# Three fp32 warm-up products in place of nine bfloat16 ones, and state buffers handed out by turn of use

## The chip, the cores and the metric

The kernel runs on one core of a Trainium2 chip. The metric is the device time of one launch in microseconds, the median of several runs. A core has a matrix engine (TensorE, PE in the profile, with PEld for its weight loads), a vector engine (VectorE, DVE), a scalar engine (ScalarE, ACT), GpSimd (POOL) and SyncE (SP), which here issues nearly all loads. They run side by side and wait for each other by semaphores; each works through its own queue in order.

## The reference, cut to what matters

Two layers: a linear attention with a decaying state, and a gated feed-forward block. B, H, S, D are 4, 8, 768, 48; the block has 3072 tokens of 384 values and 1536 hidden units.

```python
for t in range(S):
    kt, vt, rt, wt = (k[:, :, t], v[:, :, t], r[:, :, t], w[:, :, t])
    cur = np.einsum('bhd,bhe->bhde', u[None] * kt, vt)
    y[:, :, t] = np.einsum('bhd,bhde->bhe', rt, state + cur)
    state = wt[:, :, :, None] * state + np.einsum('bhd,bhe->bhde', kt, vt)
...
gate = 1.0 / (1.0 + np.exp(-(x @ w_gate)))
val = x @ w_val
return (gate * val @ w_out).astype(np.float32)
```

Here x is the attention's output with the heads of a token side by side.

## The kernel before, in words

**Attention.** The sequence is cut into six chunks of 128 steps, and a chunk of one batch entry is a group q; there are 24 groups, and group q works on batch entry q % 4 and chunk q // 4. For a group, SyncE loads a decay tile (`load_pin`, with w, k and r in lanes) and a token tile (`load_tok`, with r, v and k in rows). VectorE scans the decays and scales k and r (`prep_k`, L396 to L402; `prep_r`, L413 and L418). TensorE turns the scaled k (`turn_k`, L428), ScalarE copies it (`take_k`, L432), and ScalarE also squares the scans to watch their bounds (`guard`, L423). The scans lie in the tile `eg`, of which there is one, so the scan of the next group waits for `guard` of this one. `scores_sums` makes the scores (L447) and the sums of k and v over half chunks (L550); `mask` puts the scores into the tile `att` (L538); `state_mix` multiplies r with the states (L461) and the scores with v (L574). The bonus with u is made by GpSimd: `bonus1` (L366) and `bonus2` (L369) multiply, VectorE reduces (`bonus3`, L373), GpSimd multiplies again (`bonus4`, L386 and L387), and for the first four groups TensorE adds it to the result (`add_bonus`, L582).

**The state in two steps.** `fade` (L408) writes the state, faded to the start of a chunk, into `ready[q]`. `middle` writes the state at mid-chunk into `mid[q]` (ScalarE at L559 for the first four groups, VectorE at L561 for the others), and `keep` (L565) writes the state at the end of the chunk. `ready` and `mid` have two buffers each, made once, and a group's buffer is picked when its step is written. Readers of both are the products of `state_mix` (L461) and, for groups 12 and on, of `turned` (L484).

**Feed-forward.** The weights stay in SBUF after being taken apart into a high and a low part (`fetch`, `w_top` L286, `w_body` L297, `w_join` L301, `w_hi` L324, `w_lo` L327). `gate` and `value` (L632 and L635) make the hidden units, `sigmoid`, `hidden`, `hidden_hi` and `hidden_lo` (L646, L653, L660, L664) prepare them, and `down` or `down_turned` (L675, L679, L700) makes the output.

**Order.** The first half is written out by hand in the string ORDER: a list of steps, each of which goes to the queues of its engines in that order. Its first line is

```python
first pin0 pk0 pin1 pr0 tk0 st512 tok0 kT0 ub guard0 pk1 tok1 ss0 st256 words4 pr1 tk1 st512 m00 b1_1 m10 kT1 words0 b1_0 mid0
```

`pin0`, `tok0` and `words4` are loads; `pk0`, `pr0`, `tk0`, `kT0`, `ss0`, `b1_0` are the steps above for group 0. `first` and the steps `st512` and `st256` issue products that nobody reads (`stir`, L741), into the bank "pu". Those of `st512` and `st256` read `ends`, a tile of ones and zeros on 112 partitions; those of `first` read `blank`, a zeroed tile in the place of the tag "junk" (L267 and L268). The groups are not visited in the order of their numbers: 0 to 7, then 11, 8, 9, 10, then 12 and on, both for `fade` and for `middle`. The second half is the loop at L786, in which each of 48 steps does a block of hidden units for 512 tokens, with the next groups' work laid between.

Of the kernel before, what the change touches and what calls it, by code (L numbers as in the profile page):

```python
# [8 lines left out]
F32 = mybir.dt.float32  # L9
F32R = mybir.dt.float32r  # L10
BF16 = mybir.dt.bfloat16
# [10 lines left out]
P = 128  # L22
# [189 lines left out]
def tile_kernel(ctx: ExitStack, tc: tile.TileContext, dec: bass.AP, tok: bass.AP, wts: bass.AP, u: bass.AP, out: bass.AP):  # L212
    nc = tc.nc
# [3 lines left out]
    p1 = own.enter_context(tc.tile_pool(name="p1", bufs=1))  # L217
# [38 lines left out]
    ub = const.tile([P, DM], F32, name="ub")  # L256
# [7 lines left out]
    tiny = const.tile([1, 24], F32, name="tiny")  # L264
    nc.vector.memset(tiny, 0.0)
    nc.scalar.activation(tiny, tiny, AF.Sigmoid)
    blank = p1.tile([P, 2, 516], BF16, tag="junk", name="blank")[:, 0]  # L267
    nc.vector.memset(blank, 0.0)  # L268
    state = [const.tile([L, NP, D], F32, name=f"state{b}") for b in range(B)]

# [1 line left out]
    mids, readies = ([const.tile([L, NP * D + REST], F32, name=f"{n}{i}") for i in range(2)] for n in ("mid", "ready"))  # L272
# [57 lines left out]
    pin, tk, eg, bon, kT, att, ready, mid, bank, x, xf, gap = {}, {}, {}, {}, {}, {}, {}, {}, {}, {}, {}, {}  # L330
# [27 lines left out]
    def by_pair(t):  # L358
        return t[:, :NP * D].rearrange("a (p d) -> a p d", d=D)
# [43 lines left out]

    def fade(q):

        ready[q] = readies[q % 2]
        end = eg[q][:, 1:389:W1].unsqueeze(2).broadcast_to([L, NP, D])
        nc.vector.tensor_tensor(out=by_pair(ready[q]), in0=state[q % B], in1=end, op=ALU.mult)  # L408

# [144 lines left out]

    def middle(q):

        mid[q] = mids[q % 2]
        if q < B:
            nc.scalar.copy(by_pair(mid[q]), bank["v", q, 0])  # L559
        else:  # L560
            nc.vector.tensor_tensor(out=by_pair(mid[q]), in0=bank["v", q, 0], in1=by_pair(ready[q]), op=ALU.add)  # L561
# [65 lines left out]
    def up(s, side, n, f, i0, i1):  # L627
        t = ps1.tile([P, 512], F32, tag=side, name=f"{side}{n}_{i0}_{f}")[:, :(i1 - i0) * C]
        for k in range(NKT):
            cols = slice(s * DM + k * P, s * DM + (k + 1) * P)  # L630
            if n == 0 and (i0, f) in WHOLE:
                nc.tensor.matmul(t, lhsT=fulls[f].bitcast(F32)[:, cols], rhs=xf[n, i0][:, k], start=k == 0, stop=k == NKT - 1)  # L632
                continue
            for j, (w, a) in enumerate(((wlo, 0), (whi, 1), (whi, 0))):
                nc.tensor.matmul(  # L635
                    t, lhsT=w[f][:, cols], rhs=x[n][:, a, k, i0 * C:i1 * C], start=k == 0 and j == 0, stop=k == NKT - 1 and j == 2)
        return t
# [3 lines left out]
    def gate(n, f, i0, i1):  # L641
        hid["g", n, f, i0] = up(0, "pg", n, f, i0, i1)
# [95 lines left out]
    def stir(lhs, rhs):  # L738

        t = ps1.tile([P, 512], F32, tag="pu", name="stir")[:, :rhs.shape[1]]  # L740
        nc.tensor.matmul(t, lhsT=lhs, rhs=rhs, start=True, stop=True)  # L741

    ahead = (2, 0, 0, B)
    todo = {"ub": lambda: nc.sync.dma_start(ub, u.partition_broadcast(P)), "ahead": lambda: gate(*ahead), "first": lambda: [stir(blank[:, :P], blank[:, :512]) for _ in range(9)]}
    for cols in (256, 512,):
        todo[f"st{cols}"] = lambda cols=cols: stir(ends[:, :P], ends[:, :cols])

# [3 lines left out]
    for q in range(3 * B + 2):  # L751
        for kind, f in (
            ("pin", load_pin), ("tok", load_tok), ("b1_", bonus1), ("b2_", bonus2), ("b3_", bonus3), ("b4_", bonus4),
            ("pk", prep_k), ("fade", fade), ("pr", prep_r), ("guard", guard), ("tk", turn_k), ("kT", take_k), ("ss", scores_sums),
            ("mid", middle), ("keep", keep), ("sx", state_mix), ("yb", add_bonus), ("tx", turn_x), ("xf", plain_x), ("xh", take_x), ("xl", rest_x),
        ):
            name(f"{kind}{q}", f, q)
        for o in range(2):
            name(f"m{o}{q}", mask, q, o)
            name(f"y{o}{q}", take_y, q, o)  # L760
# [25 lines left out]
    for n in range(2, NC_):  # L786
        for f in range(NFF):
            a = (n, f, 0, B)
# [15 lines left out]
            if nxt == 3 * B + 1:  # L804
                prepare((bonus1, bonus2, prep_k, fade), nxt)
            elif nxt is not None and lag == 1:
                prepare((bonus1, bonus2), nxt)
# [12 lines left out]
            if cur is not None:  # L820
                scores_sums(cur)
                middle(cur)
                mask(cur, 0)
                mask(cur, 1)
                if cur < NG - B:
                    keep(cur)
# [13 lines left out]
            if nxt == 3 * B + 1:  # L840
                prepare((bonus3, bonus4, prep_r, guard), nxt)
            elif nxt is not None and lag == 1:
                prepare((prep_k, fade), nxt)
# [49 lines left out]
```

## Time and profile before

| what | us |
|---|---|
| median of three runs | 559.24 (558.42 to 560.91) |
| profiled execution, all of it | 559.54 |
| its span, from the first to the last instruction | 557.8 |
| TensorE busy | 543.8 |
| VectorE busy | 333.6 |
| ScalarE busy | 254.2 |
| GpSimd busy | 108.8 |

The busy time is a sum over the span; engines overlap. The page also cuts the span into 40 slices and gives the busy tenths of each engine in each. In the timeline a row gives the start in us, the duration, the engine, the line, the operation, what it writes and reads, how many are merged into it, and in brackets the idle time of the engine just before, with what ended it. A row with several products gives the time from the start of the first to the end of the last. An fp32 product of `stir` shows as two instructions.

### The profile page before, as it was taken

To read this page: it belongs to the slowest core of one execution; us is meant where nothing else is said; L and a number is where in the kernel's file an instruction comes from. 1 tells how busy PE (TensorE), PEld (TensorE's weight loads), DVE (VectorE), ACT (ScalarE), POOL (GpSimd) and SP (SyncE) were. 2 spreads that over 40 slices of the span, in tenths; PEclk is the share of its full clock that TensorE was granted. 3 is DMA by queue.
4 is the path that set the end of the run, shared out by engine and by line. 5 is a ranking of instruction groups with operands and counts; after the bars stand their busy time and mean duration, and the time that the engine had idled before them with its cause. 6 is when DMAs were issued, how large, how long until landed. Compare 5 with 4: busy or idle time off the path is not lost.

```text
span 557.8 us, 13756 instructions
## 1 busy us (share of the span) xinstructions
PE 543.8 (97%) x5875; PEld 455.5 (82%) x5875; DVE 333.6 (60%) x550; ACT 254.2 (46%) x598; POOL 108.8 (20%) x104
## 2 busy tenths in 40 slices
PE   8799999999999999999999999999999999999996
PEld 3578889999888888888888788888788888888884
DVE  6899999886634444865765665765656633321122
ACT  2556635433221323646646645645656555411221
POOL 2561520321003102331231211321311300000000
PEclk9999999999999999999999999999999999999999
DMA  8994382221310231334244344155343322100001
GB/s 292 417 386 198 144 311 87 101 101 43 115 58 1 102 139 62 116 133 141 89 147 147 113 163 162 61 164 161 116 165 120 102 65 60 63 0 2 0 1 59
DMA packets 20658, 68.46 MB, mean 123 GB/s; under 512 B 3057, under 2 KB 6769, under 8 KB 19057
## 3 DMA queue, kind: packets, MB, share of 16 engines
q1 hardware_dynamic: 17856, 63.22, 32.3%
q10 hardware_dynamic: 2736, 4.33, 2.1%
q8 instruction: 47, 0.77, 0.6%
q14 instruction: 19, 0.15, 0.1%
HBM read 61.63 MB, written 4.72 MB: 119 GB/s over the span
## 4 chain that ended last, share of the span: by engine, by line
PE 87%; DVE 5%; ACT 3%; DMA 2%; issue 1%; POOL 1%; SPq 1%; ACTq 0%; DVEq 0%; POOLq 0%
PE pg L635 24%; PE pu L635 24%; PE po L700 17%; PE po L679 7%; PE pt L484 2%; PE pa L447 2%; DMA tok<-tok 2%; PE pa L550 2%; PE po L675 1%; PE pk L428 1%; PE pa L574 1%; PE pu L632 1%; PE pa L461 1%; PE pg L632 1%; PE px L596 1%
## 5 line engine op out<-in xcount | busy, mean ns | idle before, releaser
L635 PE MATMUL pg<-x,w 128*128 128x512 f32 (+1 forms) x702 | 156.3, 367 | 0.9 <-ACT sq L317 0.7
L635 PE MATMUL pu<-x,w 128*128 128x512 f32 (+1 forms) x702 | 155.6, 366 | 0.0
L635 PEld LDWEIGHTS pg<-x,w 128*128 128x128 f32 x702 | 121.6, 188 | 23.1 <-ACT sq L317 1.1
L635 PEld LDWEIGHTS pu<-x,w 128*128 128x128 f32 x702 | 122.1, 188 | 21.7
L653 DVE TENSOR_TENSOR sg<-pu,sg 128x512 f32<-128x512 f32 (+1 forms) x84 | 51.5, 613 | 139.0 <-PE pu L635 133.4
L646 ACT ACTIVATE sg<-pg 128x512 f32<-128x512 f32 (+1 forms) x84 | 45.2, 538 | 129.5 <-PE pg L635 120.8
L660 ACT CAST hh<-sg 128x512 fp32r<-128x512 f32 (+1 forms) x75 | 42.6, 570 | 106.1 <-DVE sg L653 106.1
L700 PE MATMUL po<-hh,w 128*128 128x512 f32 x288 | 88.7, 390 | 0.0
L366 POOL TENSOR_TENSOR bon<-tok,ub 128x384 f32<-128x384 f32 x24 | 33.2, 1386 | 242.1 <-DMA tok<-tok 168.1
L664 DVE TENSOR_TENSOR hl<-sg,hh 128x512 fp32r<-128x512 f32 (+1 forms) x78 | 51.9, 671 | 41.1 <-ACT hh L660 38.7
L700 PEld LDWEIGHTS po<-hh,w 128*128 128x128 f32 x288 | 54.1, 188 | 11.0
L700 PE MATMUL po<-hl,w 128*128 128x512 f32 x144 | 57.4, 399 | 0.0
L679 PE MATMUL po<-w,hh 128*128 128x384 f32 x168 | 42.9, 336 | 0.0
L396 DVE TENSOR_TENSOR_SCAN eg<-pin,ends 112x516 f32<-112x516 f32 x24 | 33.7, 1405 | 6.2 <-DMA pin<-dec 4.3
L369 POOL TENSOR_TENSOR bon<-bon,tok 128x384 f32<-128x384 f32 x24 | 32.0, 1337 | 1.6
L700 PEld LDWEIGHTS po<-hl,w 128*128 128x128 f32 x144 | 27.0, 188 | 6.1 <-DVE hl L664 0.2
L381 POOL TENSOR_TENSOR at<-same,a 128x512 f32<-128x512 bf16 x12 | 22.2, 1851 | 44.4 <-DVE a L373 44.4
L679 PEld LDWEIGHTS po<-w,hh 128*128 128x128 f32 x168 | 30.5, 188 | 0.3
L413 DVE TENSOR_TENSOR_SCAN eg<-pin,heads 112x516 f32<-112x516 f32 x24 | 30.3, 1263 | 0.0
L423 ACT ACTIVATE junk<-eg 112x1032 bf16<-112x1032 f32 x24 | 25.5, 1061 | 8.5 <-DVE eg L413 8.5
L679 PE MATMUL po<-w,hl 128*128 128x384 f32 x84 | 29.3, 349 | 0.0
L418 DVE TENSOR_TENSOR pin<-pin,eg 112x512 f32<-112x512 f32 x24 | 25.5, 1062 | 0.8
(111 smaller groups left out, 621.2 us busy)
## 6 DMA issues: line engine op xcount, KB each, us to landing
pin<-dec SPq DMA_DIRECT2D x23, 772.0 KB, 6.1
tok<-tok SPq DMA_DIRECT2D x24, 576.0 KB, 7.3
seen<-wts SPq DMA_DIRECT2D x36, 384.0 KB, 3.1
wraw<-wts SPq DMA_DIRECT2D x12, 1151.6 KB, 10.5
y<-o ACTq DMA_DIRECT2D x10, 256.0 KB, 2.0
y<-o ACTq DMA_DIRECT2D x8, 192.0 KB, 2.0
x<-gap SPq DMA_DIRECT2D x72, 16.0 KB, 4.0
pin<-dec SPq DMA_DIRECT2D x1, 512.0 KB, 3.6
```

The source lines that it names most:

```text
L366: nc.gpsimd.tensor_tensor(out=bon[q][:, :DM], in0=tk[q][:, 0:DM], in1=ub, op=ALU.mult)
L369: nc.gpsimd.tensor_tensor(out=bon[q][:, :DM], in0=bon[q][:, :DM], in1=tk[q][:, 2 * DM:], op=ALU.mult)
L396: nc.vector.tensor_tensor_scan(out=e[:, 516:0:-1], data0=t[:, 516:0:-1], data1=ends[:, 516:0:-1], initial=0.0, op0=ALU.mult, op1=ALU.add,)
L413: nc.vector.tensor_tensor_scan(out=e[:, WW:WW + 516], data0=t[:, 0:516], data1=heads[:, 0:516], initial=0.0, op0=ALU.mult, op1=ALU.add,)
L418: nc.vector.tensor_tensor(out=rr(q), in0=rr(q), in1=er, op=ALU.mult)
L635: nc.tensor.matmul(t, lhsT=w[f][:, cols], rhs=x[n][:, a, k, i0 * C:i1 * C], start=k == 0 and j == 0, stop=k == NKT - 1 and j == 2)
L646: nc.scalar.activation(sg, hid["g", n, f, i0], AF.Sigmoid)
L653: nc.vector.tensor_tensor(out=sg, in0=hid["u", n, f, i0], in1=sg, op=ALU.mult)
L660: nc.scalar.copy(hh, hid["s", n, f, i0])
L664: nc.vector.tensor_tensor(out=hl, in0=hid["s", n, f, i0], in1=hid["hi", n, f, i0].bitcast(F32), op=ALU.subtract)
L679: nc.tensor.matmul(po[n, i][:, :DM], lhsT=h[:, c], rhs=w[f][:, 2 * DM:], start=f == 0 and j == 0, stop=f == NFF - 1 and j == 2,)
L700: nc.tensor.matmul(po[n, k], lhsT=w[f][:, cols], rhs=h, start=f == 0 and j == 0, stop=f == NFF - 1 and j == 2)
```

## The change

The tile `blank` is read as fp32: 516 words of 4 bytes on each partition, all of them cleared. `first` issues three products of 128 by 512 fp32 in place of nine of the same shape in bfloat16. `ready` and `mid` take their two buffers in turn of use, by how many groups have had one, in place of the parity of the group's number. Since group 11 is visited between 7 and 8, this changes the buffer of groups 8 to 11 alone: 11 and 9 now have buffer 0, 8 and 10 buffer 1; before it was the other way round.

```diff
-    blank = p1.tile([P, 2, 516], BF16, tag="junk", name="blank")[:, 0]
+    blank = p1.tile([P, 2, 516], BF16, tag="junk", name="blank").rearrange("a i c -> a (i c)").bitcast(F32)
     nc.vector.memset(blank, 0.0)
...
     def fade(q):
 
-        ready[q] = readies[q % 2]
+        ready[q] = readies[len(ready) % 2]
...
     def middle(q):
 
-        mid[q] = mids[q % 2]
+        mid[q] = mids[len(mid) % 2]
...
-    todo = {..., "first": lambda: [stir(blank[:, :P], blank[:, :512]) for _ in range(9)]}
+    todo = {..., "first": lambda: [stir(blank[:, :P], blank[:, :512]) for _ in range(3)]}
```

More of the change, by code (lines that the diff above doesn't have):

```diff
@@ L743, in tile_kernel @@
     ahead = (2, 0, 0, B)
-    todo = {"ub": lambda: nc.sync.dma_start(ub, u.partition_broadcast(P)), "ahead": lambda: gate(*ahead), "first": lambda: [stir(blank[:, :P], blank[:, :512]) for _ in range(9)]}
+    todo = {"ub": lambda: nc.sync.dma_start(ub, u.partition_broadcast(P)), "ahead": lambda: gate(*ahead), "first": lambda: [stir(blank[:, :P], blank[:, :512]) for _ in range(3)]}
     for cols in (256, 512,):
```

## The prediction

> **What bounds the kernel now.** I read the page first: where each engine is idle, slice by slice (a slice is 557.8/40 = 13.9 us).
>
> ```profile
> span 557.8 us, 13756 instructions
> PE 543.8 (97%) x5875; PEld 455.5 (82%) x5875; DVE 333.6 (60%) x550; ACT 254.2 (46%) x598; POOL 108.8 (20%) x104
> ...
> PE   8799999999999999999999999999999999999996
> ...
> DMA  8994382221310231334244344155343322100001
> ```
>
> TensorE is busy nearly everywhere; its 14 us of idle time lie mostly in the first two slices and the last one. The change's products run in the first slice, so what matters is which resource sets the first 30 us. The busy time by stretch (PE, PEld, DVE, ACT, POOL, granted clock, DMA share, GB/s) and then the chain of waits answer it.
>
> ```profile
> 8.00:10.00 2.00, 2.00 (x18) 0.50 (x21) 0.48 (x1) 1.48 (x3) 0.00 (x0) 1.00 0.89 168
> ...
> 16.00:18.00 2.00, 0.15 (x10) 0.15 (x10) 1.66 (x3) 1.07 (x2) 2.00 (x3) 1.00 1.00 415
> ```
>
> VectorE alone, from its start at 16.34 to TensorE's at 32.53 (busy time, granted clock, DMA share, GB/s):
>
> ```profile
> 16.34:32.53 16.19, 15.97 (x21) 1.00 1.01 420
> ```
>
> The chain of waits:
>
> ```profile
> 3.24 9.55 DMA tok<-tok
> ...
> 12.94 2.30 POOL bon L366 x2
> ...
> 15.30 1.01 POOL bon L369
> ...
> 16.34 0.55 DVE a L373
> ...
> 32.57 1.56 PE pu L632 x6
> ```
>
> The chain begins with the second token load, issued at 3.24 and landed at 12.79 because the DMA engines are full. It frees GpSimd's two bonus multiplies at 12.94, then its third at 15.30, and at 16.34 VectorE's reduction of them. From there VectorE is busy 15.97 of 16.19 us, and only then does TensorE take over. No first product stands in this chain. It stands beside it, in the timeline:
>
> ```profile
> 1.05 0.27 DVE L268 MEMSET blank<- 128x258 uint32 x1
> 1.38 5.73 PE L741 MATMUL stir<-blank 128*128 128x512 bf16 x9 [1.38 <-DVE blank L268]
> ...
> 5.09 0.66 DVE L402 TENSOR_TENSOR pin<-pin,eg 112x512 f32<-112x512 f32 x1
> 6.91 0.95 PE L428 MATMUL pk<-ident,pin 112*128 112x112 f32 x4
> 6.93 0.69 DVE L418 TENSOR_TENSOR pin<-pin,eg 112x512 f32<-112x512 f32 x1
> 7.66 1.94 PE L741 MATMUL stir<-ends 112*128 112x512 f32 x2
> 7.90 0.53 ACT L432 COPY kT<-pk 128x448 f32<-128x448 f32 x1 [5.49 <-PE pk L428]
> 8.33 1.07 ACT L423 ACTIVATE junk<-eg 112x1032 bf16<-112x1032 f32 x1
> ...
> 9.52 1.23 DVE L396 TENSOR_TENSOR_SCAN eg<-pin,ends 112x516 f32<-112x516 f32 x1 [1.89 <-ACT junk L423]
> 11.60 0.60 PE L428 MATMUL pk<-ident,pin 112*128 112x112 f32 x4
> 12.04 1.04 PE L741 MATMUL stir<-ends 112*128 112x512 f32 x2
> 12.72 0.69 DVE L418 TENSOR_TENSOR pin<-pin,eg 112x512 f32<-112x512 f32 x1
> 14.13 0.36 DVE L565 TENSOR_TENSOR state<-pa,mid 112x192 f32<-112x192 f32 x1
> 16.34 0.55 DVE L373 TENSOR_REDUCE a<-bon 128x8 f32<-128x384 f32 x1 [1.85 <-POOL bon L369]
> 17.85 0.36 PE L574 MATMUL pa<-tok,at 64*32 64x48 f32 x11 [1.93 <-issue]
> ```
>
> Here is a second path: the ninth product ends at 7.11, the transposes of group 0 (pk) could have begun at 5.75 when L402 ended but begin at 6.91, ScalarE copies them (kT), runs the bounds square of L423 behind that, and VectorE waits 1.89 us for it, since there is one eg buffer. So the first products do hold VectorE's group 1. But that path ends at 14.49 with the state update of L565, and VectorE then sits idle for 1.85 us until GpSimd's multiply. Those 1.85 us are the cover of the whole edit.
>
> **The change, part by part.**
>
> The blank memset. Before, it clears 258 words a partition in 0.27 us; now it clears 516, twice as many, so 0.27 x 516/258 = 0.55. The first product starts about 0.27 later, at 1.65. VectorE's first operation that the first products could hold up, L402, comes at 5.09, so only TensorE feels it.
>
> The first products. Nine bfloat16 ones go: 5.73 us. Three fp32 ones of 512 columns come; the nearest rows are the existing stirs on ends, of the same type and length, each of which shows as two instructions. One takes 1.94 us at 7.66 and 1.04 us at 12.04. The same instruction at two speeds means that the array is still slow at 7.66, though the granted clock reads 1.00 in the 8 to 10 row. Ends: if the three run at the slow rate, 3 x 1.94 = 5.82, ending at 7.47, 0.36 later than 7.11. If they all ran fast, 3 x 1.04 = 3.12, ending at 4.77; then pk starts at 5.75, when its data is there, takes 0.60 in place of 0.95, kT runs 6.4 to 6.9, the square cannot start before the scan that it reads is done, just ahead of L418 at 6.93, and VectorE's second scan follows the square's start by 9.52 - 8.33 = 1.19 as now, so at 8.12 in place of 9.52: 1.40 earlier. I take the slow end, since the slow row is the nearest in time (7.66, against 12.04), and treat the path as 0.36 later.
> [...]
>
> What lies behind it. The late end moves VectorE's L565 end from 14.49 to 14.85, 1.49 us before the multiply that it waits for next; the early end moves it to 13.09 and the idle time grows to 3.2. Both cost or bring 0. If that cover were gone, the price would be the shift itself: +0.36 or -1.40. TensorE's six fewer instructions of loads and products (18 become 12) move the place where it starves at 16 to 18 us (the 1.93 us before the last 11 products of L574, attributed to issue), by six instructions. That place is under VectorE's gapless work too. SP's queue: the change issues no DMA; SP's third decay load waits for TensorE's L461 and moves with it, as the next rows show, and the weight loads queue behind it.
>
> ```profile
> 15.23 0.33 SPq L341 DMA_DIRECT2D pin<-dec  x1
> ...
> 24.55 1.23 DVE L396 TENSOR_TENSOR_SCAN eg<-pin,ends 112x516 f32<-112x516 f32 x1
> ```
>
> Its reader starts at 24.55 without a wait, 9.3 us after the issue, and the DMA share at 16 to 18 is 1.00, so an issue 0.4 later or 1.4 earlier keeps its place in a full line: 0. GpSimd's queue gets nothing new.
>
> GpSimd beside VectorE. The only way in which the shift touches the chain is through the two multiplies of 12.94 to 15.24, which overlap L418 and VectorE's next operations. Their durations (least, median, most, in ns):
>
> ```profile
> L366 POOL TENSOR_TENSOR bon<-tok,ub x24: 995/1278/1992, 12.9 to 436.1; 128x384 f32<-128x384 f32 x24
> ```
> ```profile
> L369 POOL TENSOR_TENSOR bon<-bon,tok x24: 998/1339/2607, 15.3 to 437.8; 128x384 f32<-128x384 f32 x24
> ```
>
> The pair takes 2.30. At the minimum it would be 1.99 (-0.31), at the maximum 3.98 (+1.68). A VectorE path 0.36 later overlaps about as much as before, so I take 0 and keep both for the range.
>
> The state buffers. mid and ready now take turns in the order in which groups are visited (0 to 7, then 11, 8, 9, 10, 12 on), so group 11 no longer takes the buffer of group 7, nor 12 that of 10. What that could remove is a wait of fade (L408) or middle (L561) for products of the group before:
>
> ```profile
> L408 DVE TENSOR_TENSOR ready<-state,eg x20: 344/352/1169, 50.0 to 438.1; 112x192 f32<-112x192 f32 x20
> its engine sat idle before it (us, times) until:
> who waited for it (us, times):
> ```
> ```profile
> 204.47 0.35 DVE L408 TENSOR_TENSOR ready<-state,eg 112x192 f32<-112x192 f32 x1
> ```
> ```profile
> 202.43 0.22 PE L461 MATMUL pa<-mid,pin 48*64 48x48 f32 x2
> ```
> ```profile
> DVE mid L561 <- PE pa L550: 6.8, 11, 2.5
> ```
>
> The list of what L408 waited for is empty. Group 11's, at 204.47, comes 1.8 us after the last reader of the old buffer (202.65). The waits of L561 are for L550, the products that it takes in, and none is for L461, the readers of a buffer. So nothing is removed, and behind group 12 both rules give the same parity: 0. What is late next is what was late before.
>
> **Sum.** 0 (memset and products under 1.85 us of cover) + 0 (GpSimd pair) + 0 (buffers) = 0 against the profiled execution, 557.8 of span and 559.54 in all, which lies 0.30 above the median of 559.24. I predict the median, 559.2.
>
> **The rivals.** The faster one: the early end is real and the chain is wrong about what holds VectorE at 16.34, so that the 1.40 us carry through, with 0.31 of GpSimd's pair: 559.2 - 1.7 = 557.5. For it speaks the 1.89 us wait of VectorE for ScalarE, which the first products cause; against it, that the wait is followed by the 1.85 us one for GpSimd, whose own wait is for a load in a full DMA. It is 0.3%, still under what would count as faster; for that 2.8 us would have to go, and TensorE's path holds no more than 1.40.
>
> The slower one: VectorE's displaced two-input operations collide with GpSimd's multiplies on the chain. It decides from the first overlap, as the pair is on the chain without slack. At their maxima the pair costs 1.68 more and the third multiply 2.61 - 1.01 = 1.60 more: 559.2 + 3.3 = 562.5, 0.6% slower. For it speak the spread of those rows; against it, that VectorE is idle during the third multiply now and would still be, and that a shift of 0.36 keeps the pair's overlap.
> [...]
>
> A third: TensorE starves longer at 16 to 18 us because its instructions end elsewhere. The products that follow (L582) go to ScalarE, whose copy of them stands ahead of its cast of a weight (L324), and that cast feeds VectorE's L327:
>
> ```profile
> 20.28 0.81 PE L582 MATMUL pa<-bon,ident 128*128 128x192 f32 x4
> ...
> 21.03 1.16 ACT L324 CAST w<-full 128x1152 fp32r<-128x1152 f32 x1
> ...
> 22.61 1.35 DVE L327 TENSOR_TENSOR w<-full,w 128x1152 fp32r<-128x1152 f32 x1
> ```
>
> ScalarE's cast ends at 22.19 and VectorE needs it at 22.61, so it decides from 0.42 us on; a starving time twice as long gives 1.93 - 0.42 = +1.5, 560.7. Nothing makes six instructions cost that much, so it is unlikely.
>
> **How the numbers follow.** About 0.5% of 559.2, 2.8 us, is what a measurement of this kernel can tell from no change; its three runs alone lie between 558.42 and 560.91. No change: 0.80, 558.2 to 560.2. Faster rival: 0.10, at 557.5. Third: 0.05, at 560.7. Collision: 0.05, at 562.5. The range 557.4 to 560.8 takes in all but the last and some spread of the runs. Over 0.5% faster (under 556.4): 0.05, from a faster rival with a fast set of runs; over 0.5% slower (above 562.0): 0.05, the collision; within: 0.90.
>
> **What the profile would show.** Right: three pairs of fp32 products from 1.65 to about 7.4 (or earlier, if they run fast), pk and the square moved by the same, VectorE's idle time before 16.34 changed by the opposite amount, the second token load landing near 12.8, and TensorE's first long stretch beginning near 32.5. L408 and L561 lie as before. Wrong: if GpSimd's pair starts at 12.9 but VectorE's reduction does not start near 16.3, or if the second token load lands at another time than 12.8, or if TensorE's slow rate outlives 10 us and VectorE's group 1 comes more than 1.85 us late.

## The result and the profile after

The changed kernel takes 563.03 us (median of seven runs, 561.57 to 563.96) against 559.24 (seven runs, 558.42 to 562.21). The ratio is 1.0056, 95% interval 1.0032 to 1.0079: slower by about 3 us (3.8 by the two medians), and outside the predicted range. Its profiled execution took 562.21 with a span of 560.4, against 559.54 and 557.8, so the two traces hold about 2.6 us of the loss. Single runs spread: of 75 runs of the kernel before that were timed beside the experiments, the 8 with a mean granted clock under 0.9935 have a median of 562.1 us and the 49 at 0.9965 or more one of 559.0, and all seven of the changed kernel lie between 0.991 and 0.996.

The page of the changed kernel:

```profile
span 560.4 us, 13750 instructions
...
PE   7789999999999999999999999999999999999996
...
PEclk9899999999999999999999999999999999999999
```

TensorE lost a tenth in the first slice and in the third and, new, the granted clock dips in the second (14.0 to 28.0 us). Behind that TensorE's digits are as before. The chain of waits of the changed kernel shows what stands there now (start, duration, what):

```profile
14.45 0.61 PE pa L461 x15
15.05 0.73 PE pa L574 x56
15.78 3.66 issue
19.44 0.29 PE pa L574 x7
19.73 1.55 PE stir L741 x2
21.28 0.04 issue
21.33 2.07 PE stir L741 x2
23.40 0.49 PE pa L582 x2
...
23.92 0.32 ACT bon L587
24.24 1.06 ACT w L324
...
32.42 1.96 DVE eg L396
...
36.10 1.56 PE pu L632 x6
```

Before, the chain went through the token load, GpSimd and VectorE here. Now it goes through TensorE: a hole of 3.66 us, then warm-up products that nobody reads, then the bonus products, ScalarE's cast, VectorE. The timeline of the changed kernel, to be read against the rows shown before:

```profile
1.10 0.49 DVE L268 MEMSET blank<- 128x516 f32 x1
1.65 5.67 PE L741 MATMUL stir<-blank 128*128 128x512 f32 x6 [1.65 <-DVE blank L268]
7.16 0.55 PE L428 MATMUL pk<-ident,pin 112*128 112x112 f32 x4
7.54 1.04 PE L741 MATMUL stir<-ends 112*128 112x512 f32 x2
9.36 1.23 DVE L396 TENSOR_TENSOR_SCAN eg<-pin,ends 112x516 f32<-112x516 f32 x1 [1.61 <-ACT junk L423]
12.56 0.69 DVE L418 TENSOR_TENSOR pin<-pin,eg 112x512 f32<-112x512 f32 x1
12.71 2.35 POOL L366 TENSOR_TENSOR bon<-tok,ub 128x384 f32<-128x384 f32 x2 [8.53 <-DMA tok<-tok]
13.31 0.70 PE L447 MATMUL pa<-pin 48*64 48x64 f32 x32 [0.39 <-DVE pin L418]
16.18 0.55 DVE L373 TENSOR_REDUCE a<-bon 128x8 f32<-128x384 f32 x1 [1.85 <-POOL bon L369]
19.44 0.29 PE L574 MATMUL pa<-tok,at 64*32 64x48 f32 x8 [3.66 <-issue]
19.66 3.74 PE L741 MATMUL stir<-ends 112*128 112x512 f32 x4
23.20 1.01 PE L582 MATMUL pa<-bon,ident 128*128 128x192 f32 x4
24.13 1.16 ACT L324 CAST w<-full 128x1152 fp32r<-128x1152 f32 x1
25.32 1.36 DVE L327 TENSOR_TENSOR w<-full,w 128x1152 fp32r<-128x1152 f32 x1 [2.79 <-ACT w L324]
```

Up to 16.2 us VectorE's and GpSimd's rows agree with those of before within 0.25 us. Then TensorE is without instructions for 3.66 us in place of 1.93. The warm-up products behind the hole stood like this before, in the timeline and in the stretches (PE, PEld, DVE, ACT, POOL, granted clock, DMA share, GB/s):

```profile
18.14 2.31 PE L741 MATMUL stir<-ends 112*128 112x512 f32 x4
```
```profile
18.00:20.00 2.00, 1.94 (x15) 0.78 (x8) 2.00 (x4) 1.25 (x1) 2.00 (x3) 1.00 1.00 423
20.00:22.00 2.00, 2.00 (x56) 1.51 (x58) 1.90 (x4) 1.23 (x3) 1.43 (x2) 1.00 1.04 431
```

They now hold up the bonus products by 23.20 - 19.66 = 3.54 in place of 20.28 - 18.14 = 2.14, because the clock has dropped; the stretches of the changed kernel show it:

```profile
18.00:20.00 2.00, 0.56 (x9) 0.45 (x9) 2.00 (x4) 0.56 (x1) 2.00 (x3) 1.00 1.01 420
20.00:22.00 2.00, 1.94 (x3) 0.50 (x2) 1.90 (x4) 0.71 (x1) 1.27 (x2) 0.54 1.02 429
22.00:24.00 2.00, 2.00 (x6) 1.05 (x4) 0.53 (x1) 0.08 (x1) 0.00 (x0) 0.60 0.98 408
```

The sum: the hole ends 1.52 later at the first warm-up product (19.66 against 18.14), the products there cost 1.40 more, so the bonus products start 2.92 later. ScalarE's cast starts 3.10 later (24.13 against 21.03); VectorE had 0.42 to spare for it, which leaves 2.68, and VectorE is seen to wait 2.79. The span grew by 2.6. That the 2.68 comes near this is in part luck. A later scan of `eg` by VectorE takes 0.81 longer, 1.96 in the chain above (at 32.42) against this row in the chain of before:

```profile
29.70 1.15 DVE eg L396
```

So TensorE's long stretch begins 36.10 - 32.57 = 3.53 later. About 1 us of that is won back between 100 and 400 us, in part because waits of TensorE that the kernel before has there (0.7 and twice 0.2) are gone and only one of 0.3 is new. Why the scan was slower is not shown; GpSimd's multiply beside it took 2.19 in place of 1.90.

Why is the hole longer? The records of the DMA queue that carries instructions hold 47 packets of 16 KB beside 11,837 TensorE records in the kernel before, one for every 252; below, a block is what one such packet brings. Around the hole there is one such packet, the first of that queue. The row of that queue (packets, MB, share of the 16 engines) in the kernel before, in the stretch 15 to 16 us:

```profile
q8 instruction: 1, 0.02, 6.2%
```

and of the changed kernel in the stretch 17 to 18 us:

```profile
q8 instruction: 1, 0.02, 6.4%
```

By the trace's times the packet starts at 15.40 before and at 17.11 after, 1.71 later. Counted in order of time from 0, TensorE's instruction behind the hole is number 449 in both, and it starts 2.45 and 2.33 us after the packet does. In the kernels below this distance is 2.29 to 2.45, and 2.93 in e11. From this near-constant distance I take the starving to be a wait for a block of code, and the block comes later after the change.

### The profile page after: what moved, and what is told of

Its sections match the earlier page's. It is cut to its first block, busy times and chain, and to the rows that moved or that the text cites. A ratio compares the mean times of both kernels' runs of the same rounds, so it can differ in the third digit from the quotient of the medians.

```text
span 560.4 us, 13750 instructions
## 1 busy us (share of the span) xinstructions
PE 544.1 (97%) x5872; PEld 456.0 (81%) x5872; DVE 333.2 (59%) x550; ACT 253.6 (45%) x598; POOL 109.2 (19%) x104
## 4 chain that ended last, share of the span: by engine, by line
PE 89%; ACT 4%; DVE 3%; issue 2%; DMA 2%; ACTq 0%; SPq 0%; DVEq 0%
PE pg L635 25%; PE pu L635 24%; PE po L700 16%; PE po L679 8%; PE pa L447 2%; PE pt L484 2%; PE pa L550 2%; PE pa L574 2%; PE po L675 1%; PE pk L428 1%; PE pa L461 1%; PE pu L632 1%; PE pg L632 1%; PE stir L741 1%; DMA x<-gap 1%
## 5 line engine op out<-in xcount | busy, mean ns | idle before, releaser
L366 POOL TENSOR_TENSOR bon<-tok,ub 128x384 f32<-128x384 f32 x24 | 31.7, 1322 | 239.1 <-DMA tok<-tok 173.3
L396 DVE TENSOR_TENSOR_SCAN eg<-pin,ends 112x516 f32<-112x516 f32 x24 | 37.8, 1574 | 6.1 <-DMA pin<-dec 4.5
L369 POOL TENSOR_TENSOR bon<-bon,tok 128x384 f32<-128x384 f32 x24 | 34.0, 1420 | 1.6
L418 DVE TENSOR_TENSOR pin<-pin,eg 112x512 f32<-112x512 f32 x24 | 25.5, 1061 | 0.8
```

The costliest lines, as they stand in the source:

```text
L366: nc.gpsimd.tensor_tensor(out=bon[q][:, :DM], in0=tk[q][:, 0:DM], in1=ub, op=ALU.mult)
L369: nc.gpsimd.tensor_tensor(out=bon[q][:, :DM], in0=bon[q][:, :DM], in1=tk[q][:, 2 * DM:], op=ALU.mult)
L396: nc.vector.tensor_tensor_scan(out=e[:, 516:0:-1], data0=t[:, 516:0:-1], data1=ends[:, 516:0:-1], initial=0.0, op0=ALU.mult, op1=ALU.add,)
L418: nc.vector.tensor_tensor(out=rr(q), in0=rr(q), in1=er, op=ALU.mult)
```

## The experiments

Three theories. Count: the changed kernel has six TensorE instructions fewer ahead of this place, and that moves the point at which the next block is asked for behind a wait. Time: the fp32 products shift TensorE, and the instruction load falls behind another load. Buffers: the other half of the edit.

**One half of the change at a time.**

```diff
 # e1_products_only: the new first products, and
-        ready[q] = readies[len(ready) % 2]
+        ready[q] = readies[q % 2]
-        mid[q] = mids[len(mid) % 2]
+        mid[q] = mids[q % 2]
```

> Three fp32 products in place of nine bfloat16 ones; the state buffers by parity as before. Count theory (six fewer TensorE instructions put the place where the next instruction block is asked for behind TensorE's wait for VectorE, so the block comes later, TensorE starves 3.7 us in place of 1.9, its clock drops, and the products behind run slowly) and time theory (the fp32 products shift TensorE in time, and the instruction fetch falls behind a load): both about 1.0055 of before, 562.3 us, with the starving time near 3.7. Buffer theory (the new turn of the state buffers is what costs): 1.000, 559.2.

562.6 us, 1.0045 (1.0025 to 1.0066); starving 3.71 us.

```diff
 # e2_buffers_only: nine bfloat16 products, and
-        ready[q] = readies[q % 2]
+        ready[q] = readies[len(ready) % 2]
-        mid[q] = mids[q % 2]
+        mid[q] = mids[len(mid) % 2]
```

> The state buffers by turn of use, the nine bfloat16 products as before. Count theory and time theory: 1.000 of before, 559.2 us, starving time 1.9 us as before. Buffer theory: about 1.0055, 562.3.

559.78 us, 0.9999 (0.9980 to 1.0018). The buffers cost and bring nothing; the products carry the loss. The starving was 0.91 in place of the 1.9 expected: in this execution L418 of group 1 took 1.51 in place of 0.69, so TensorE came to the hole later, while the packet came as early (15.24). The length of one hole thus also varies from execution to execution; the packet's time is the better sign.

**Count against time.** The first gives the changed kernel its six instructions back, the second takes six from the kernel before.

```diff
 # e3_pad6, on the changed kernel (zeros is the bfloat16 view of blank)
-"first": lambda: [stir(blank[:, :P], blank[:, :512]) for _ in range(3)]
+"first": lambda: [stir(blank[:, :P], blank[:, :512]) for _ in range(3)] + [stir(zeros[:, :P], zeros[:, :16]) for _ in range(3)]
```

> The changed kernel with three bfloat16 products of 16 columns behind the three fp32 ones, so that TensorE has as many instructions ahead of group 1 as before (six more than in the changed kernel). They read zeros and nobody reads them. Count theory: the starving time falls back to about 1.9 us, the clock does not drop, and the time is 0.999 to 1.000 of before, about 559. Time theory: the fp32 products and the early clock stay, so the starving time stays near 3.7 and the time at 1.0055, 562.3.

560.2 us, 1.0007 (0.9984 to 1.0029). Three more useless products undo the loss. Its timeline (one added line of code makes L574 into L575, and so on):

```profile
17.96 0.36 PE L575 MATMUL pa<-tok,at 64*32 64x48 f32 x11 [0.85 <-issue]
18.25 2.31 PE L742 MATMUL stir<-ends 112*128 112x512 f32 x4
20.40 0.81 PE L583 MATMUL pa<-bon,ident 128*128 128x192 f32 x4
```

The hole is 0.85 us, the warm-up products run fast, and the bonus products start at 20.40, as they did before (20.28). This run alone would not separate the theories, since the three products also delay VectorE's L402 of group 1, from 11.39 to 12.12.

```diff
 # e4_six_bf16, on the kernel before
-... for _ in range(9)]
+... for _ in range(6)]
```

> The kernel before with six of its nine bfloat16 products: six TensorE instructions fewer, as in the changed kernel, but no fp32 products, and the products end about 1.9 us sooner. Count theory: starving time near 3.7 us and 1.005 of before, about 562. Time theory: the starving time stays near 1.9 and the time at 1.000 or a little below, 558.5 to 559.3.

562.26 us, 1.0028 (1.0005 to 1.0050), with no fp32 product in `first`. That is less than the 1.005 that the count theory gave: three of the twelve runs lie between 559.4 and 559.8 us, the other nine between 560.5 and 563.1. Its timeline:

```profile
18.62 0.29 PE L574 MATMUL pa<-tok,at 64*32 64x48 f32 x8 [2.85 <-issue]
18.84 3.63 PE L741 MATMUL stir<-ends 112*128 112x512 f32 x4
24.50 1.36 DVE L327 TENSOR_TENSOR w<-full,w 128x1152 fp32r<-128x1152 f32 x1 [2.17 <-ACT w L324]
```

The same picture as the changed kernel, 0.8 us sooner: hole, slow warm-up products, VectorE waiting. The time theory falls with these two and with the next pair.

**Where the threshold lies.** One or two products of 16 columns in place of e3's three, then eight or seven bfloat16 products in place of nine. In TensorE instructions that is two (e7) or four (e8) more than in the changed kernel, and two (e9) or four (e10) fewer than in the kernel before. If the count alone decides, e8 and e9 go together, and so do e7 and e10.

> The changed kernel with one bfloat16 product of 16 columns behind the three fp32 ones: two TensorE instructions more. [...] Count theory: the block is asked for either as early as before (packet near 15.5, starving time 1 to 2 us, 559 us) or as late as in the changed kernel (packet near 17, starving time 3.7, 562 us), and nothing between, by how far ahead instructions are taken in. Time theory: as the changed kernel, 562.

> [...] Count theory: packet near 15.5 and 559 us, or near 17 and 562 us, and not later than with one product. Time theory: as the changed kernel, 562.

562.14 and 559.44 us, one execution each. The hole of e7_pad2 and then of e8_pad4:

```profile
19.49 0.29 PE L575 MATMUL pa<-tok,at 64*32 64x48 f32 x9 [3.44 <-issue]
```
```profile
18.07 0.33 PE L575 MATMUL pa<-tok,at 64*32 64x48 f32 x10 [1.01 <-issue]
```

Two more instructions, given by one product of 16 columns, bring the packet 1.3 us sooner and shorten the hole by 2.4. The two times differ by 2.7 us, but as single executions they show little: the kernel before alone lies between 557.7 and 562.1 in the same comparison.

> [...] Count theory: packet near 15.3, at most 1.9 us of starving, clock not dropped, 559 us. [...]

> [...] Count theory: packet after 16.2, starving time 2.8 to 3.7 us, 561 to 562 us, although the products end 1.3 us sooner. Otherwise as with eight: 559.

558.93 and 559.53 us, one execution each. Eight did nearly as expected (packet at 14.92, 1.99 of starving). Seven met half of it: the packet came late, at 16.10, but the starving was 1.75 in place of 2.8 to 3.7, and this one time was not longer. Its rows say why:

```profile
12.53 1.94 PE L741 MATMUL stir<-ends 112*128 112x512 f32 x2
...
18.44 0.29 PE L574 MATMUL pa<-tok,at 64*32 64x48 f32 x9 [1.75 <-issue]
```

At 12.53 the array still ran slowly (1.94 for the pair that takes 1.04 elsewhere), so TensorE itself reached the hole later and found the block nearer.

The kernels side by side, with three that follow below (e5, e6 and e12, which is e9 once more). The first column counts TensorE's instructions ahead of the first product of L447 for group 1; "released" is the end of VectorE's operation named, by its row:

| kernel | ahead | released by, at | packet starts | between | starving |
|---|---|---|---|---|---|
| before | 181 | L402, 11.54 | 15.40 | 3.86 | 1.93 |
| e2 buffers only | 181 | L402, 11.54 | 15.24 | 3.70 | 0.91 |
| e3 three small | 181 | L402, 12.12 | 15.67 | 3.55 | 0.85 |
| e8 two small | 179 | L402, 12.06 | 15.78 | 3.72 | 1.01 |
| e6 before, no warm-up pair | 181 | L402, 11.53 | 15.26 | 3.73 | 1.15 |
| e9 eight | 179 | L402, 10.90 | 14.92 | 4.02 | 1.99 |
| e12 eight again | 179 | L402, 10.89 | 14.41 | 3.52 | 1.45 |
| e7 one small | 177 | L418, 13.52 | 17.07 | 3.55 | 3.44 |
| e10 seven | 177 | L418, 12.54 | 16.10 | 3.56 | 1.75 |
| after | 175 | L418, 13.25 | 17.11 | 3.86 | 3.66 |
| e1 products only | 175 | L418, 13.15 | 17.02 | 3.87 | 3.71 |
| e5 after, no warm-up pair | 175 | L418, 12.75 | 16.93 | 4.18 | 4.08 |
| e4 six | 175 | L418, 12.71 | 16.29 | 3.58 | 2.85 |

The packet starts 3.52 to 4.18 us after one of two events: with 179 or more ahead, after L402 releases the transposes of group 1; with 177 or fewer, after L418 releases its scores. So, by these times, the block is asked for as TensorE's queue passes about its 178th instruction. With 179 ahead that one still belongs to the warm-up product between transposes and scores and goes out with the transposes; with 177 it belongs to the scores and is held until VectorE is done with L418, 1.86 us later in the changed kernel (13.25 against 11.39). The asking itself has no record; where it falls is my estimate from the times of the release and of the packet. How long the hole lasts hangs on when TensorE comes to it too, so the last column does not follow the packet alone.

**What makes a block take 3.8 us, and what the late products cost.**

```diff
 # e11_late_words, on the changed kernel's ORDER
-kT1 words0 b1_0 ... b3_0 words1 sx0 st512 st512 mid1 ... yb0 pin2 b4_1
+kT1 b1_0 ... b3_0 sx0 st512 st512 mid1 pin2 words0 words1 ... yb0 b4_1
```

> The changed kernel with two of its weight loads (words0 and words1, 1.15 MB each) issued behind the third decay load, which moves ahead of the fourth one's steps, so that the DMA engines run dry after about 15.5 us in place of being full. The block of instructions is asked for at about 13.3 as in the changed kernel. Theory that the full DMA makes the fetch take 3.8 us: the packet comes 1 to 2 us after the asking, at 14.5 to 15.7, and starving falls below 2 us. Theory that a fetch takes that long by itself: packet near 17.1, starving 3.7. The time is read only from the fetch; the total is worse than 562 in both, since the weights come later.

563.16 us, one execution; the packet starts at 14.79, 1.29 after L418 ends at 13.50, and the hole is 1.69. The stretches (PE, granted clock, DMA share, GB/s) show the emptied DMA:

```profile
13.00:14.00 1.00, 0.61 (x29) 1.00 0.59 249
14.00:15.00 1.00, 1.00 (x66) 1.00 0.20 62
15.00:16.00 1.00, 1.00 (x66) 1.00 0.02 9
```

The same asking, 2.6 us faster (1.29 against 3.86 in the changed kernel, where the share from 13 to 18 us reads 0.98 to 1.03). I take it that in the other kernels the code waits behind data in the full DMA engines; it rests on this one execution.

```diff
 # e5_no_stirs, on the changed kernel; e6_before_no_stirs does the same to the kernel before
-... sx0 st512 st512 mid1 ...
+... sx0 mid1 ...
```

> The changed kernel without the two fp32 warm-up products that stand right behind the starving place (the pair of 512 columns between the mixing products of group 0 and its bonus). They read constants and nobody reads them; they stand behind instruction 449, so the fetch is as late as in the changed kernel: starving time 3.7 us. Theory that the loss is the starving time itself: TensorE is back at 19.4 as before this edit, and the time stays near 1.004, above 561.5. Theory that the loss comes from these products, which run at the dropped clock between the late block and the bonus products: the bonus products start at 19.9 to 20.3 in place of 23.2, VectorE does not wait for its weight, and the time is 0.999 to 1.001 of before, 559 to 560.

560.99 us, 1.0029 (1.0008 to 1.0050), between the two. The rows of the profiled execution (562.97):

```profile
19.35 0.39 PE L574 MATMUL pa<-tok,at 64*32 64x48 f32 x8 [4.08 <-issue]
19.82 1.65 PE L582 MATMUL pa<-bon,ident 128*128 128x192 f32 x4
22.53 1.35 DVE L327 TENSOR_TENSOR w<-full,w 128x1152 fp32r<-128x1152 f32 x1
31.08 1.23 DVE L396 TENSOR_TENSOR_SCAN eg<-pin,ends 112x516 f32<-112x516 f32 x1 [1.45 <-ACT junk L423]
```

A hole of 4.08 us, and yet the bonus products start at 19.82 and VectorE does not wait for its weight: the hole's own cost went to nothing there, as the second theory had it. Its forecast of 559 to 560 us was missed all the same, and so was the first theory's of 561.5 or more. Without those products the clock is still down at 24 to 26 us, where the changed kernel has 1.00 again, and VectorE waits 1.45 at 31.08. The stretch in e5 (length, PE, granted clock, DMA share, GB/s):

```profile
24.00:26.00 2.00, 2.00 (x9) 0.56 0.86 290
```

This execution also had a wait late in the run, which the next row shows and which differed from 0 to 2.0 us between the profiled executions of this study, whatever the kernel; it may widen all these intervals, and the total of e5 can't be split beyond that.

```profile
PE pg L635 <- DMA x<-gap: 2.0, 1, 2.0
```

> The kernel before without the same two products. The starving time of 1.9 us stays. If VectorE sets the stretch from 16.3 to 32.5 us, it brings nothing: 0.999 to 1.001, 559.2. If the bonus products that they hold up by 0.4 us matter, it brings up to 0.4 us, 558.8.

559.62 us, 1.0007 (0.9993 to 1.0021): nothing, as expected. Its trace bears on e5: with a hole of only 1.15 us and a wait of 1.51 for GpSimd soon behind it, the bonus products take 1.65 at 19.54 and again at 23.58 here too, as they do in e5 (0.81 and 0.92 in the kernel before), and VectorE's scan waits the same 1.45, at 30.80. So in e5 this slow stretch and this wait need no late block; they come where the pair is missing, and e6 as a whole pays nothing for them. What leaves e5 above e6 (1.0029 against 1.0007) is not shown.

**A better version?**

> The kernel with eight bfloat16 products once more, timed in rounds, since its one look was 0.9 us below its neighbour. Count theory with the stretch from 16 to 32 us set by VectorE: the block comes 0.5 us sooner than before, but no wait on the chain goes; only GpSimd's and VectorE's start at 16.1 in place of 16.3 is kept, so 0.999 to 1.000 of before. If the sooner block itself pays, 0.998 or less.

The kernel before with eight of its nine products, timed in twelve runs: 560.38 us, 1.0017 (0.9998 to 1.0037), no gain. None of these kernels beats the one before.

## Why the prediction was wrong, by its own steps

- **The state buffers: right.** No wait goes and none comes (0.9999).
- **The memset: right in kind**, 0.49 in place of 0.55.
- **The first products: the wrong way, at no cost.** I took the slow rate for all three, 1.94 each, ending at 7.47. They ended at 7.32, which is near by luck: the first two took 2.13 each (1.65 to 5.91), the third 1.41. The transposes behind them ran in 0.55 in place of 0.95, and VectorE's group 1 came 0.16 earlier (9.36) and not 0.36 later. The array was fast earlier than before here: the next pair ran in 1.04 (7.54) and not in 1.94.
- **The cover up to 16.3: right.** VectorE waited 1.85 us for GpSimd as before; token load, GpSimd's pair (2.35) and the reduction at 16.18 lie where they were forecast. The collision did not come there; the scan that ran 0.81 longer at 32.42 stood in no term.
- **"That place is under VectorE's gapless work too": wrong, and it decided.** The step on the six instructions said that the starving place moves by six instructions. It did not move (449 in both); the packet that brings its block moved, behind a wait, by 1.71 us. The cover there was the 0.42 us between ScalarE's cast and VectorE's L327, which I had worked out under the third rival and not here.
- **The third rival: the right mechanism, given 0.05, and under-priced.** "Nothing makes six instructions cost that much" is the sentence that failed. It priced a doubled hole at 1.93 - 0.42 = +1.5. Measured: the hole 1.73 longer, of which 1.52 arrive at its end, plus 1.40 from the dropped clock in the warm-up products, minus 0.42, so about 2.5 to 2.7, beside VectorE's wait of 2.79. The term of the clock was missing, and so was the slower scan behind it.

The row that should have stopped me was quoted in the prediction: 1.93 us put down to issue. I treated a hole without a cause as a constant. The traces show the hole in front of the first block that a packet brings, in all kernels here, 0.85 to 4.08 us long.

## What to carry to other kernels

A hole in TensorE's queue that the profile puts down to issue may be a wait for code: look for the instruction packet near it (here it starts 2.29 to 2.93 us ahead of the instruction behind the hole) and for the DMA share at that time. Where loads fill the DMA, adding or taking away a few instructions far ahead can move the asking across a wait and cost more than the instructions themselves (two of them, e7 against e8: the packet 1.3 us later, the hole 2.4 us longer), so compare instruction counts ahead of such a hole, and not only durations. And warm-up products are dear where they stand behind a hole after which the clock drops (1.40 us more here), though without them the clock stayed down longer (e5: 0.56 from 24 to 26 us, against 1.00 in the changed kernel).

## What the runs showed of the hardware

A refill of TensorE's code took 3.52 to 4.18 us from the release by which the asking is told to the packet, with the DMA engines full (share 0.98 to 1.03 in the changed kernel), and 1.29 with the share at 0.59 and then 0.20 (e11, one execution). After the hole of 3.66 us in the changed kernel the granted clock read 0.54 and 0.60 in two stretches of 2 us (20 to 24 us), which at half speed (0.50 is the reading of e5 from 20 to 24 us) makes 1.84 + 1.60 = 3.44 us of slow clock. TensorE's slow rate at the start outlasted the bfloat16 products: with seven of them, which ran for 4.45 us from 1.38 on, a pair at 12.53 still took 1.94 in place of 1.04, 11 us after the first product. Why it lasted so long, no run here shows.
